# Attention with a top-32 mask and a gated expert layer: a different way to split double weights, and two weight pairs carried over from chunk to chunk

## Chip, cores and metric

One core of one Trainium2 chip. The metric is the device time of one execution in microseconds, the median of the runs.

## What is computed

```python
scores = scale * np.matmul(q, k.transpose(0, 1, 3, 2))        # 4 batches, 8 heads, 576 x 576, head size 64
kth = np.partition(scores, -32, axis=-1)[..., -32:-31]
scores = np.where(scores >= kth, scores, -1000000000.0)
attn = softmax(scores); x = attn @ v                          # 2304 tokens x 512
out = ((x @ w_a) * (x @ w_b)) @ w_out                         # 512 -> 1536 -> 512
```

The inputs q, k, v are float32; the three weight matrices are 64-bit doubles and reach the chip as such.

## The kernel before

**Matmuls.** A float32 product is made of fp32r products: each operand is split into a high part h (fp32r) and a low part l, and h·h + h·l + l·h are added in PSUM. Activations are split with a ScalarE copy (h) and a GpSimd subtraction (l).

**Attention.** The 2304 tokens are taken in 8 chunks (256 or 320 tokens of one batch), each chunk in 4 pairs of heads, each pair in 4 or 5 tiles of 128 query rows: 144 tiles. Per tile: TensorE makes the scores (L499, or L505 to L510), ScalarE copies half or all of them to SBUF (L526, L528), VectorE finds the 32 largest of each row with eight-at-a-time maxima (L535 to L545), ScalarE takes the exponential (L557, L570), the mask comes from VectorE (L559) or from a TensorE product (L568), the row is divided by its sum (p, L577 on GpSimd or L575 on ScalarE), TensorE transposes p (L601), ScalarE and GpSimd split it (L608 to L617), and TensorE multiplies by v (L647 to L662). From `SCALAR_SCALE` on, every even tile takes L575 in place of L577.

**Experts.** `up` makes, for a chunk, 24 products of x with a weight tile w (12 pairs of w_a and w_b; L697 to L699, 12 matmuls each); the pair is multiplied and split into gh and gl (L706 to L717). `down` makes 4 products with the 12 tiles of w_out, which stay in SBUF (L727 to L729, 36 matmuls each). A chunk's `up` and `down` are mixed with the attention of the chunk behind it; the last chunk's stand at the end.

**Conversion of the weights.** Each of the 36 weight tiles (128 x 512 doubles) goes once through `convert`: two loads of 512 KB, the raw words (L430, `raw`) and the same shifted by two bytes (L431, `alt`); two ScalarE Relu copies of the high words (L451, L452) that GpSimd adds (L453); VectorE shifts the bits in place and cuts them to h (L449), takes the next bits from `alt` (L449 again) and the exponent alone (L456); ScalarE writes h (L457) and turns the next bits into a float (L458); GpSimd multiplies it by the exponent's power of two, which is l (L459). The 24 tiles of w_a and w_b are then written to DRAM (`wd`, L461) and loaded again for every chunk (L693) through 4 buffers `w`. Of the first chunk, the tiles from `CONV_FIRST` on are used right where they were converted. Scratch of a conversion is three slots of the 12 that w_out's tiles take later (or slots of kx, qx, ptl, or a piece of gh or gl).

**Order.** No engine's order is written by hand. Each operation goes to a planner (`Plan`) with an engine, a cost in us and a key; the planner plays the program through with these costs and emits each engine's operations in the order in which they started there, the smallest key first among those ready. The keys of attention are the tile's number, of conversion `CONV_AT + CONV_STEP * k`, of experts late ones. All DMAs are issued in one queue on SP, in order. Where TensorE would stand still in the plan, the planner puts a filler matmul of 256 columns in (L288, `still`), up to a number of columns per stretch.

Line numbers here and in the profile are those of the kernel before.

Of the kernel before, what the change touches and what calls it, by code (L numbers as in the profile page):

```python
# [246 lines left out]
def attn_moe(ctx: ExitStack, tc, qT, kT, v, wa, wb, wo, out):  # L247
# [43 lines left out]
        return Buf(pool, shape, dtype, tag, bufs)  # L291

    def act(n, fn, r, w, ps=False, ptr=0, k=None):
        plan.op("ACT", n / 1200 + (0.065 if ps else 0.093) + 0.093 * ptr, key[0] if k is None else k, fn, r, w)

    def dve(n, fn, r, w, cost=None, k=None):
        plan.op("DVE", cost or (n + 66) / 960, key[0] if k is None else k, fn, r, w)

    def pool(n, fn, r, w, cost=None):
        plan.op("POOL", cost or 0.2 + n / 480, key[0], fn, r, w)  # L300

    def pe(cols, fn, r, w, rows=1.0, num=0, k=None):
        plan.op("PE", cols / 2353 + 0.009 * num, key[0] if k is None else k, fn, r, w, rows=rows)
# [104 lines left out]
    def convert(j, i):  # L408

        src = wo[j] if i == 2 else (wa, wb)[i][j].rearrange("p k e -> p (k e)")
        n = 2 * NJ + j if i == 2 else 2 * j + i
        if i == 2 and j in CONV_AWAY:
            raw, alt = buf([128, 1024], U4, "kx", 2), buf([128, 1024], U4, "ptl", 2)
            tmp, low = buf([128, 512], U4, "qx", 2), buf([128, 512], U4, "qx", 2)
            plan.enlist(raw, alt, tmp, low)
        elif n < CONV_FIRST and n % CONV_BIG == CONV_BIG - 1:
            big = buf([128, 3840], U4, ("gh", "gl")[n // CONV_BIG % 2], 1)  # L420
            raw, alt, tmp, low = [Part(big, *x) for x in ((0, 1024), (1024, 1024), (2048, 512), (2560, 512))]
        else:
            while i == 2 and len(listed) + 1 + 3 * sum(x not in CONV_AWAY for x in range(len(listed), j + 1)) > NJ:
                plan.enlist(fin[len(listed)])
                listed.append(fin[len(listed)])
            raw, alt, both = [buf([128, 1024], U4, "wo", NJ, const) for _ in range(3)]
            tmp, low = Part(both, 0, 512), Part(both, 512, 512)
            plan.enlist(raw, alt, both)
        first = [PR[0]["kr"], PR[0]["qr"]]
        dma(524e3, lambda: nc.sync.dma_start(raw[:, :], src.bitcast(U4)), [], [raw], after=first)  # L430
        dma(524e3, lambda: nc.sync.dma_start(alt[:, :].bitcast(U2)[:, 1:2048], src.bitcast(U2)[:, 0:2047]), [], [alt], after=first)  # L431
        if i == 2:
            w = fin[j]
            if j == NJ - 1:
                plan.enlist(*fin)
        else:
            w = buf([128, 2, 4, 128], FR, "w", 4)

        def odd(x):
            return x[:, :].rearrange("p (n t) -> p n t", t=2)[:, :, 1]  # L440

        def part(k):
# [5 lines left out]
        def bits(out, x, by, keep, how):  # L448
            return vec.tensor_scalar(out, x, by, keep, op0=how, op1=OP.bitwise_and)  # L449

        act(512, lambda: nc.scalar.activation(f(tmp), odd(raw).bitcast(FT), AF.Relu, scale=2.0 ** -116), [raw], [tmp])  # L451
        act(512, lambda: nc.scalar.activation(f(low), odd(raw).bitcast(FT), AF.Relu, scale=-2.0 ** -84), [raw], [low])  # L452
# [66 lines left out]
    def topk(i, s):  # L519

        alone = vector_mask(i)
        sb = buf([128, 2, HS], FT, "sb", 2)
        if alone:
            act(S, lambda: nc.scalar.activation(sb.ap, s[:, :, 0:HS], AF.Copy), [s], [sb], ps=True)  # L526
# [12 lines left out]

        def eight(r):  # L540
            return tb[:, g, 8 * r:8 * r + 8] if r else t8.ap
        for r in range(4):
            dve(HS + 8, lambda r=r: vec.max(eight(r), mx[:, g]), [(mx, g, 0), (mx, g, 1)], [tk[r]])  # L543
            if r < 3:
                dve(HS + 8, lambda r=r: vec.match_replace(mx[:, g], eight(r), mx[:, g], LOW), [tk[r]], [(mx, g, 0), (mx, g, 1)], 0.44)  # L545
            if r == 0:
                act(1, lambda: nc.scalar.activation(bias.ap, t8[:, 0:1], AF.Copy, scale=-0.125), [t8], [bias], k=URGENT)
        if g == GRP - 1:
            pool(g, lambda: nc.gpsimd.tensor_tensor(short[:, i - g:i + 1], tb[:, :, 31], mx[:, :, HS + 7], OP.subtract),
                 [(mx, x, y) for x in range(GRP) for y in (0, 1)] + [(tb, x, 3) for x in range(GRP)], [("short", i)])  # L550
        return bias, (tb, g, tk[3]), sb

    def softmax(i, s, found):
        bias, (tb, g, tok), sb = found
        pt, sm = buf([128, 2, HS], FT, "p", 2), buf([128, 2], FT, "sm", 3)
        if vector_mask(i):
            act(S, lambda: nc.scalar.activation(pt.ap, sb.ap, AF.Exp, bias=bias.ap, scale=0.125),  # L557
                [sb, bias], [pt], ptr=1)
            dve(S, lambda: vec.scalar_tensor_tensor(pt.ap, sb.ap, tb[:, g, 31:32], pt.ap, op0=OP.is_ge, op1=OP.mult,  # L559
                                                    accum_out=sm[:, 0:1]), [sb, tok], [pt, sm], 0.95)  # L560
# [120 lines left out]

    G, A, O = {}, {}, {}

    def up(c, j, which):
        n = chunks[c][2]
        xh, xl = X[c]
        if (c, j, which) in direct:
            w = direct.pop((c, j, which))
            wt = [(w, 0), (w, 1)]
        else:  # L690
            w = buf([128, 2, 4, 128], FR, "w", 4)
# [50 lines left out]
    for i, t in enumerate(tiles):  # L742
# [23 lines left out]
        if c == 0:  # L766
# [6 lines left out]
            for j in range(NJ):  # L773
                key[0] = ATTENTION + CONV_AT + 2 * NJ * CONV_STEP + CONV_LAST * j
                convert(j, 2)
                key[0] = EXPERTS
                while k < CONV_FIRST * (j + 1) / NJ:
                    up(c, k // 2, k % 2)
# [149 lines left out]
```

## Time and profile before

| | us |
|---|---|
| median of 3 runs | 931.04 (927.84 to 936.62) |
| the profiled execution, whole | 930.03 |
| its span, first to last instruction | 928.1 |
| TensorE busy in the span | 862.6 (of it fillers 66.7) |
| VectorE busy | 771.2 |
| ScalarE busy | 702.2 |
| GpSimd busy | 599.4 |

The span falls into four stretches. Up to about 25 us the first tiles start. From 25 to 250 us the weights are converted beside the attention of the first tiles. From 250 to 850 us attention and experts run mixed. Behind 850 us are left the `down` of the last but one chunk and the `up` and `down` of the last. The tables of stretches give, for each engine, busy microseconds and the number of instructions, then the clock that TensorE was granted as a share, the mean busy share of the 16 DMA engines and what they moved.

### The profile page before, as it was taken

How to read it: one execution, taken by the hardware profiler on the slowest of the kernel's cores; microseconds unless marked ns; L12 is line 12 of the kernel's file. 1: busy time of each engine (PE TensorE's matmuls, PEld its weight loads, DVE VectorE, ACT ScalarE, POOL GpSimd, SP SyncE). 2: the span in 40 equal slices, each digit the busy share in tenths (PEclk: the TensorE clock that was granted, in tenths of full speed). 3: DMA queues.
4: the chain of work that ended last, by engine and by line, in shares of the span. 5: the costliest groups of instructions: out<-in, count | busy, mean ns of one | idle time of the engine just before them, and what ended most of it. 6: DMA issues, size and time to landing. Idle time of an engine off the chain costs nothing.

```text
span 928.1 us, 18959 instructions
## 1 busy us (share of the span) xinstructions
PE 862.6 (93%) x5893; PEld 762.4 (82%) x5893; DVE 771.2 (83%) x2390; ACT 702.2 (76%) x1618; POOL 599.4 (65%) x706
## 2 busy tenths in 40 slices
PE   6887989999899899989998999988999999999998
PEld 3454557576789899988898999987999989999987
DVE  5889989989699899989998999989999989992010
ACT  4687878998877888878897888887888877772220
POOL 3365657877767777767777786777777786762120
PEclk8898989999999999999999999999999999999999
DMA  8698877987548884578548884689467774673580
GB/s 277 249 303 315 293 267 282 310 301 273 143 105 250 254 272 101 173 262 256 151 126 237 261 276 125 195 270 256 124 211 215 254 193 114 206 225 105 188 281 27
DMA packets 101581, 202.52 MB, mean 218 GB/s; under 512 B 17761, under 2 KB 55649, under 8 KB 101473
## 3 DMA queue, kind: packets, MB, share of 16 engines
q1 hardware_dynamic: 101472, 201.24, 68.8%
q8 instruction: 49, 0.80, 0.4%
q14 instruction: 60, 0.48, 0.2%
HBM read 157.93 MB, written 17.30 MB: 189 GB/s over the span
## 4 chain that ended last, share of the span: by engine, by line
PE 50%; DVE 14%; DMA 12%; ACT 10%; POOL 8%; issue 4%; SPq 2%; POOLq 0%; ACTq 0%; DVEq 0%
PE mm L697 6%; PE tp L601 6%; DMA w<-wd 5%; PE mm L699 5%; PE mm L698 5%; PE mm L727 4%; PE mm L729 4%; PE mm L728 4%; DVE mx L545 3%; DVE top L543 2%; POOL ptl L615 2%; PE mm L660 2%; DMA wo<-wa 2%; PE mm L288 2%; PE s L499 2%
## 5 line engine op out<-in xcount | busy, mean ns | idle before, releaser
L697 PE MATMUL mm<-xh,w 128*128 128x256 f32 (+1 forms) x768 | 240.3, 313 | 16.8 <-DMA w<-wd 9.4
L699 PE MATMUL mm<-xh,w 128*128 128x256 f32 (+1 forms) x768 | 228.1, 297 | 0.3 <-POOL w L459 0.3
L698 PE MATMUL mm<-xl,w 128*128 128x256 f32 (+1 forms) x768 | 228.1, 297 | 0.0
L615 POOL TENSOR_TENSOR ptl<-e,pth 128x512 fp32r<-128x512 f32 (+1 forms) x126 | 151.9, 1209 | 80.7 <-ACT e L613 65.7
L543 DVE MAX8 top<-mx 128x8 f32<-128x296 f32 x432 | 194.8, 457 | 2.0
L697 PEld LDWEIGHTS mm<-xh,w 128*128 128x128 f32 x768 | 146.1, 190 | 29.0 <-issue 8.9
L699 PEld LDWEIGHTS mm<-xh,w 128*128 128x128 f32 x768 | 146.1, 190 | 0.5 <-POOL w L459 0.5
L698 PEld LDWEIGHTS mm<-xl,w 128*128 128x128 f32 x768 | 146.4, 191 | 0.0
L545 DVE MATCH_REPLACE8 mx<-top,mx 128x296 f32<-128x296 f32 x288 | 129.5, 450 | 0.1
L608 ACT ACTIVATE pth<-tp 128x640 fp32r<-128x640 f32 (+3 forms) x160 | 102.5, 649 | 24.9 <-PE tp L601 23.1
L717 POOL TENSOR_TENSOR gl<-a,gh 128x256 fp32r<-128x256 f32 (+1 forms) x96 | 78.5, 819 | 62.4 <-ACT gh L716 59.3
L727 PE MATMUL mm<-gh,wo 128*128 128x256 f32 (+1 forms) x384 | 117.4, 306 | 0.5 <-ACT b L733 0.5
L601 PE MATMUL tp<-ident,p 128*128 128x128 f32 x720 | 107.0, 280 | 10.5 <-POOL p L577 4.3
L729 PE MATMUL mm<-gh,wo 128*128 128x256 f32 (+1 forms) x384 | 113.6, 296 | 0.0
L728 PE MATMUL mm<-gl,wo 128*128 128x256 f32 (+1 forms) x384 | 113.5, 296 | 0.0
L577 POOL TENSOR_SCALAR p<-p,sm 128x576 f32<-128x576 f32 x87 | 72.4, 832 | 54.5 <-DVE sm L573 46.4
L601 PEld LDWEIGHTS tp<-ident,p 128*128 128x128 f32 x720 | 83.4, 142 | 25.4 <-POOL p L577 12.3
L711 DVE TENSOR_TENSOR a<-mm,a 128x320 f32<-128x320 f32 (+1 forms) x84 | 38.4, 458 | 64.9 <-PE mm L699 63.5
L535 DVE TENSOR_TENSOR mn<-s,sb 128x288 f32<-128x288 f32 x144 | 64.2, 446 | 24.6 <-ACT sb L528 19.0
L613 ACT ACTIVATE e<-tp 128x640 f32<-128x640 f32 x113 | 79.6, 704 | 4.6 <-POOL pth L617 4.2
L727 PEld LDWEIGHTS mm<-gh,wo 128*128 128x128 f32 x384 | 72.7, 189 | 1.6 <-ACT b L733 0.7
L728 PEld LDWEIGHTS mm<-gl,wo 128*128 128x128 f32 x384 | 72.8, 190 | 0.0
(124 smaller groups left out, 2218.7 us busy)
## 6 DMA issues: line engine op xcount, KB each, us to landing
w<-wd SPq DMA_DIRECT2D x182, 512.0 KB, 4.7
wd<-w SPq DMA_DIRECT2D x24, 512.0 KB, 5.5
kr<-kT SPq DMA_DIRECT2D x24, 288.0 KB, 3.3
kx<-kh SPq DMA_DIRECT2D x48, 144.0 KB, 2.6
kx<-kr SPq DMA_DIRECT2D x48, 144.0 KB, 4.3
vr<-v SPq DMA_DIRECT2D x25, 256.0 KB, 4.0
wo<-wa SPq DMA_DIRECT2D x12, 512.0 KB, 7.4
wo<-wa SPq DMA_DIRECT2D x12, 511.8 KB, 8.0
```

The costliest lines, as they stand in the source:

```text
L543: dve(HS + 8, lambda r=r: vec.max(eight(r), mx[:, g]), [(mx, g, 0), (mx, g, 1)], [tk[r]])
L545: dve(HS + 8, lambda r=r: vec.match_replace(mx[:, g], eight(r), mx[:, g], LOW), [tk[r]], [(mx, g, 0), (mx, g, 1)], 0.44)
L601: nc.tensor.transpose(tp[:, kb, :], pf[:, k0:k0 + 128], ident)
L608: act(640 // len(dst), lambda bh=bh, to=to, fr=fr: nc.scalar.activation(bh[:, :, to], tp[:, :, fr], AF.Copy), [tp], [(bh, i)], ps=True)
L613: act(640, lambda: nc.scalar.activation(e.ap, tp.ap, AF.Copy), [tp], [e], ps=True)
L615: pool(512 // len(dst), lambda bh=bh, bl=bl, to=to, fr=fr: nc.gpsimd.tensor_tensor(bl[:, :, to], e[:, 0:4, fr], bh[:, 0:4, to].bitcast(FT) ...
L697: mm(ps[:, :n], w[:, 0, kb, :], xh[:, kb, :n], start=(kb == 0), stop=False)
L698: mm(ps[:, :n], w[:, 0, kb, :], xl[:, kb, :n], start=False, stop=False)
L699: mm(ps[:, :n], w[:, 1, kb, :], xh[:, kb, :n], start=False, stop=(kb == 3))
L727: mm(ps[:, :n], fin[j][:, 0, ms], gh[:, j, :n], start=(j == 0), stop=False)
L728: mm(ps[:, :n], fin[j][:, 0, ms], gl[:, j, :n], start=False, stop=False)
L729: mm(ps[:, :n], fin[j][:, 1, ms], gh[:, j, :n], start=False, stop=(j == NJ - 1))
```

## The change

Three things change, and with them the planner's numbers.

1. In `convert`, the shifted copy `alt` and its load are gone. VectorE only shifts (L454 of the changed kernel) and takes the exponent alone into `low` (L455); ScalarE writes h (L456); GpSimd subtracts h from the shifted value W (L457); VectorE multiplies the next 16 bits, read as 16-bit integers from the raw words, by 2^-36 and the exponent's power of two (L458); GpSimd adds both (L459). Scratch is two slots of 12 in place of three.
2. `up` keeps the w tiles of the last two pairs of a chunk (`KEEP`), and the next chunk begins with these pairs; the order of pairs turns around from chunk to chunk.
3. The division of even tiles goes to ScalarE from tile 80 on, before from tile 30 on. Sixteen tiles of the first chunk, before 14, are loaded again from DRAM.

```diff
-SCALAR_SCALE = 30
+SCALAR_SCALE = 80
-CONV_FIRST = 14
+CONV_FIRST = 16
-TURN, WEIGH, SPLIT = 1.5, 0, -2
-CONV_AT, CONV_STEP, CONV_LAST = -1, 1.4, 1
+TURN, WEIGH, SPLIT = 1.5, 1, -4
+CONV_AT, CONV_STEP, CONV_LAST = -1, 1.7, 0.5
...
-        plan.op("DVE", cost or (n + 66) / 960, key[0] if k is None else k, fn, r, w)
+        plan.op("DVE", cost or (n + 76) / 960, key[0] if k is None else k, fn, r, w)
-        plan.op("SP", nbytes / 345e3, key[0], fn, r, w, num=num, inner=inner, after=after)
+        plan.op("SP", nbytes / 310e3, key[0], fn, r, w, num=num, inner=inner, after=after)
...
-        dma(524e3, lambda: nc.sync.dma_start(alt[:, :].bitcast(U2)[:, 1:2048], src.bitcast(U2)[:, 0:2047]), [], [alt], after=first)
...
-        dve(0, lambda: bits(tmp[:, :], tmp[:, :], 3, 0xFFFFF000, OP.logical_shift_left), [], [tmp], 0.4)
-        dve(0, lambda: bits(low[:, :], odd(alt), 4, 0x1FFFFF, OP.logical_shift_right), [alt], [low], 0.4)
-        dve(0, lambda: vec.tensor_scalar(alt[:, 0:512], tmp[:, :], 0xFF800000, None, op0=OP.bitwise_and), [tmp], [alt], 0.4)
-        act(512, lambda: nc.scalar.activation(part(0), f(tmp), AF.Copy, scale=2.0 ** 32), [tmp], [(w, 0)])
-        act(512, lambda: nc.scalar.activation(f(low), low[:, :], AF.Copy), [], [low])
-        pool(512, lambda: nc.gpsimd.tensor_tensor(part(1), alt[:, 0:512].bitcast(FT), f(low), OP.mult), [alt, low], [(w, 1)])
+        dve(0, lambda: vec.tensor_scalar(tmp[:, :], tmp[:, :], 3, None, op0=OP.logical_shift_left), [], [tmp], 0.58)
+        dve(0, lambda: vec.tensor_scalar(low[:, :], tmp[:, :], 0xFF800000, None, op0=OP.bitwise_and), [tmp], [low], 0.54)
+        act(512, lambda: nc.scalar.activation(part(0), f(tmp), AF.Copy), [tmp], [(w, 0)])
+        pool(512, lambda: nc.gpsimd.tensor_tensor(f(tmp), f(tmp), part(0).bitcast(FT), OP.subtract), [(w, 0)], [tmp])
+        dve(0, lambda: vec.scalar_tensor_tensor(f(low), upper(raw), 2.0 ** -36, f(low), op0=OP.mult, op1=OP.mult), [raw], [low], 0.68)
+        pool(512, lambda: nc.gpsimd.tensor_tensor(part(1), f(tmp), f(low), OP.add), [tmp, low], [(w, 1)])
...
+        elif (j, which) in kept:
+            w = kept.pop((j, which))
+            wt = [w]
...
+        if last and c + 1 < len(chunks):
+            kept[j, which] = w
...
-            for j in range(NJ):
+            first = sorted({j for j, _ in kept}, reverse=c % 2 == 1)
+            rest = sorted(set(range(NJ)) - set(first), reverse=c % 2 == 1 and c > 1)
+            for n, j in enumerate(first + rest):
                 for which in range(2):
-                    up(c, j, which)
+                    up(c, j, which, n >= NJ - KEEP)
```

What this makes of the order is shown at three places. First VectorE, before, around the thirteenth tile: the three VectorE steps of one conversion (`wo_1241` is its scratch, `wo_1154` its shifted load) between the top-32 steps of a tile.

```order
L449 TENSOR_SCALAR wo_1241<-wo_1241 128x512
L543 MAX top_1202<-mx_1159 128x8
L449 TENSOR_SCALAR wo_1241<-wo_1154 128x512
L545 MATCH_REPLACE mx_1159<-top_1202,mx_1159 128x296
L456 TENSOR_SCALAR wo_1154<-wo_1241 128x512
```

The same in the changed kernel, near the same tile (`wo_1297` is the scratch, `wo_1228` the raw words).

```order
L454 TENSOR_SCALAR wo_1297<-wo_1297 128x512
L545 MATCH_REPLACE mx_1280<-t8_1399,mx_1280 128x296
L455 TENSOR_SCALAR wo_1297<-wo_1297 128x512
L543 MAX top_1343<-mx_1280 128x8
L573 RECIPROCAL sm_1412<-sm_1412 128x1
L458 SCALAR_TENSOR_TENSOR wo_1297<-wo_1228,wo_1297 128x512
```

Three VectorE steps stay three; the last of them now reads two SBUF tensors. Second GpSimd, before, around the fifteenth tile, where L577 is the division of p that a tile's transposes wait for, and L453 and L459 are conversion.

```order
L577 TENSOR_SCALAR p<-p,sm 128x576
L459 TENSOR_TENSOR w<-wo 128x512
L453 TENSOR_TENSOR wo<-wo 128x512
L577 TENSOR_SCALAR p<-p,sm 128x576
L459 TENSOR_TENSOR w<-wo 128x512
L549 TENSOR_TENSOR short<-top,mx 128x2
L453 TENSOR_TENSOR wo<-wo 128x512
L459 TENSOR_TENSOR w<-wo 128x512
L577 TENSOR_SCALAR p<-p,sm 128x576
```

And in the changed kernel, around the fourteenth tile, where L453, L457 and L459 are conversion.

```order
L577 TENSOR_SCALAR p<-p,sm 128x576
L457 TENSOR_TENSOR wo<-wo,w 128x512
L453 TENSOR_TENSOR wo<-wo 128x512
L459 TENSOR_TENSOR w<-wo 128x512
L549 TENSOR_TENSOR short<-top,mx 128x2
L457 TENSOR_TENSOR wo<-wo,w 128x512
L453 TENSOR_TENSOR wo<-wo 128x512
L577 TENSOR_SCALAR p<-p,sm 128x576
L459 TENSOR_TENSOR w<-wo 128x512
L457 TENSOR_TENSOR wo<-wo,w 128x512
L453 TENSOR_TENSOR wo<-wo 128x512
L459 TENSOR_TENSOR w<-wo 128x512
```

Between the two divisions shown there stand five steps of conversion; before two, then three. Third the DMA queue of SP, before, where the second chunk's `up` ends: the loads of w0 and w1 (`wd0_0` to `wd1_1`) for the third chunk stand between the loads of attention (kx, vr, kr).

```order
L309 DMA kx_4706<-kh_4696 64x576 x2
L309 DMA w_4716<-wd0_0_68 128x1024
L309 DMA kx_4706<-kr_4509 64x576 x2
L309 DMA w_4769<-wd0_1_69 128x1024
L324 DMA vr_4798<-v 128x4x128
L326 DMA vr_4798<-v 64x128 x2
L309 DMA w_4808<-wd1_0_70 128x1024
L309 DMA w_4836<-wd1_1_71 128x1024
L318 DMA kr_4857<-kT 128x576
```

In the changed kernel, at the same place, behind the second chunk's last two loads of w.

```order
L311 DMA w_4665<-wd11_0_90 128x1024
L311 DMA w_4726<-wd11_1_91 128x1024
L326 DMA vr_4756<-v 128x4x128
L328 DMA vr_4756<-v 64x128 x2
L320 DMA kr_4767<-kT 128x576
L311 DMA mid_96<-qh_4460 64x64 x4
L311 DMA mid_96<-qr_4344 64x64 x2
L322 DMA qr_4928<-qT 128x320
L326 DMA vr_5021<-v 128x4x128
L328 DMA vr_5021<-v 64x128 x2
```

No load of w stands there; the third chunk's first one comes 28 rows later, behind the four stores of the chunk's result.

## Rows read from the trace of the kernel before

**Rows 1.** Busy time of each engine, four stretches (start:end, length first)
```profile
core 0: us, PE busy (x) PEld busy (x) DVE busy (x) ACT busy (x) POOL busy (x), PEclk, DMA share, GB/s
25.00:250.00 225.00, 202.98 (x1125) 136.95 (x1122) 202.94 (x576) 190.25 (x444) 149.54 (x156) 0.96 0.79 276
250.00:850.00 600.00, 573.12 (x4181) 548.47 (x4182) 550.79 (x1763) 489.25 (x1123) 433.02 (x522) 0.99 0.68 202
850.00:865.00 15.00, 15.00 (x104) 15.00 (x104) 0.00 (x0) 0.88 (x2) 0.00 (x0) 1.00 0.09 34
865.00:905.00 40.00, 36.31 (x289) 34.89 (x288) 4.67 (x11) 9.63 (x24) 8.10 (x11) 1.00 0.79 267
```

**Rows 2.** The same stretches, the filler matmuls alone (PE, PEld)
```profile
25.00:250.00 225.00, 49.87 (x264) 24.62 (x261) 0.96 0.79 276
250.00:850.00 600.00, 9.60 (x52) 4.76 (x52) 0.99 0.68 202
```

**Rows 3.** Waits of TensorE, 250 to 928 us: total, times, longest
```profile
PE mm L697 <- DMA w<-wd: 9.2, 12, 1.6
PE tp L601 <- ACT e L613: 3.6, 3, 2.0
PE s L568 <- ACT r L563: 3.1, 3, 2.2
PE s L509 <- ACT p L570: 2.7, 2, 2.1
PE mm L697 <- ACT a L706: 2.2, 3, 1.2
PE tp L601 <- POOL p L577: 2.0, 5, 0.6
...
PEld tp L601 <- POOL p L577: 7.2, 19, 0.8
...
PEld mm L697 <- DMA w<-wd: 2.7, 2, 1.5
```

**Rows 4.** Waits of VectorE, 25 to 250 us
```profile
DVE mn L535 <- ACT sb L528: 9.3, 13, 2.0
DVE sm L573 <- ACT sm L572: 6.6, 7, 2.1
```

**Rows 5.** Groups on VectorE by shape (count, busy us, mean ns)
```profile
L559 DVE SCALAR_TENSOR_TENSOR p<-sb,top,p 128x576 f32<-128x576 f32 x63 | 62.8, 997 | 0.4 <-issue 0.3
L449 DVE TENSOR_SCALAR wo<-wo 128x512 uint32<-128x512 uint32 x52 | 32.4, 633 | 3.4 <-POOL wo L453 3.4
L456 DVE TENSOR_SCALAR wo<-wo 128x512 uint32<-128x512 uint32 x26 | 15.3, 587 | 0.0
```

**Rows 6.** Single lines on VectorE: shortest, median, longest ns
```profile
L559 DVE SCALAR_TENSOR_TENSOR p<-sb,top,p x63: 786/849/2225, 261.2 to 836.0; 128x576 f32<-128x576 f32 x63
L449 DVE TENSOR_SCALAR wo<-wo x52: 402/420/1536, 17.4 to 223.9; 128x512 uint32<-128x512 uint32 x52
L449 DVE TENSOR_SCALAR qx<-ptl x8: 408/752/1492, 36.3 to 244.9; 128x512 uint32<-128x512 uint32 x8
L535 DVE TENSOR_TENSOR mn<-s,sb x144: 427/447/459, 7.0 to 827.4; 128x288 f32<-128x288 f32 x144
```

**Rows 7.** Groups on GpSimd and ScalarE by shape
```profile
L577 POOL TENSOR_SCALAR p<-p,sm 128x576 f32<-128x576 f32 x87 | 72.4, 832 | 54.5 <-DVE sm L573 46.4 <-DMA wo<-wb 5.1 <-DMA kx<-kh 1.2
L459 POOL TENSOR_TENSOR w<-wo 128x512 fp32r<-128x512 f32 x22 | 28.1, 1277 | 19.1 <-ACT wo L458 7.0 <-DVE top L543 6.6 <-DVE sm L573 1.9
L575 ACT ACTIVATE p<-p,sm 128x576 f32<-128x576 f32 x57 | 44.2, 775 | 4.7 <-DVE sm L573 4.3
L458 ACT ACTIVATE wo<-wo 128x512 f32<-128x512 uint32 x26 | 16.2, 624 | 2.3 <-DVE wo L449 2.2
```

**Rows 8.** DMA issues: count, KB each, median us to landing
```profile
w<-wd SPq DMA_DIRECT2D x182, 512.0 KB, 4.7
...
wo<-wa SPq DMA_DIRECT2D x12, 512.0 KB, 7.4
wo<-wa SPq DMA_DIRECT2D x12, 511.8 KB, 8.0
```

More of the change, by code (lines that the diff above doesn't have):

```diff
@@ L21 @@
 LO, HI = 256, 320
+W_BUFS = 4
+KEEP = 2
 GRP = 2
@@ L293, in act @@
     def act(n, fn, r, w, ps=False, ptr=0, k=None):
-        plan.op("ACT", n / 1200 + (0.065 if ps else 0.093) + 0.093 * ptr, key[0] if k is None else k, fn, r, w)
+        plan.op("ACT", n / 1200 + (0.085 if ps else 0.11) + 0.075 * ptr + 0.035 * (n == 1), key[0] if k is None else k, fn, r, w)
     def dve(n, fn, r, w, cost=None, k=None):
-        plan.op("DVE", cost or (n + 66) / 960, key[0] if k is None else k, fn, r, w)
+        plan.op("DVE", cost or (n + 76) / 960, key[0] if k is None else k, fn, r, w)
     def pool(n, fn, r, w, cost=None):
@@ L302, in pe @@
     def pe(cols, fn, r, w, rows=1.0, num=0, k=None):
-        plan.op("PE", cols / 2353 + 0.009 * num, key[0] if k is None else k, fn, r, w, rows=rows)
+        plan.op("PE", cols / 2300 + 0.009 * num, key[0] if k is None else k, fn, r, w, rows=rows)
     def dma(nbytes, fn, r, w, num=1, inner=False, after=()):
-        plan.op("SP", nbytes / 345e3, key[0], fn, r, w, num=num, inner=inner, after=after)
+        plan.op("SP", nbytes / 310e3, key[0], fn, r, w, num=num, inner=inner, after=after)
     def move(dst, src):
@@ L415, in convert @@
         if i == 2 and j in CONV_AWAY:
-            raw, alt = buf([128, 1024], U4, "kx", 2), buf([128, 1024], U4, "ptl", 2)
-            tmp, low = buf([128, 512], U4, "qx", 2), buf([128, 512], U4, "qx", 2)
-            plan.enlist(raw, alt, tmp, low)
+            raw, tmp, low = buf([128, 1024], U4, "kx", 2), buf([128, 512], U4, "qx", 2), buf([128, 512], U4, "qx", 2)
+            plan.enlist(raw, tmp, low)
         elif n < CONV_FIRST and n % CONV_BIG == CONV_BIG - 1:
             big = buf([128, 3840], U4, ("gh", "gl")[n // CONV_BIG % 2], 1)
-            raw, alt, tmp, low = [Part(big, *x) for x in ((0, 1024), (1024, 1024), (2048, 512), (2560, 512))]
+            raw, tmp, low = [Part(big, *x) for x in ((0, 1024), (1024, 512), (1536, 512))]
         else:
-            while i == 2 and len(listed) + 1 + 3 * sum(x not in CONV_AWAY for x in range(len(listed), j + 1)) > NJ:
+            while i == 2 and len(listed) + 1 + 2 * sum(x not in CONV_AWAY for x in range(len(listed), j + 1)) > NJ:
                 plan.enlist(fin[len(listed)])
                 listed.append(fin[len(listed)])
-            raw, alt, both = [buf([128, 1024], U4, "wo", NJ, const) for _ in range(3)]
+            raw, both = [buf([128, 1024], U4, "wo", NJ, const) for _ in range(2)]
             tmp, low = Part(both, 0, 512), Part(both, 512, 512)
-            plan.enlist(raw, alt, both)
+            plan.enlist(raw, both)
         first = [PR[0]["kr"], PR[0]["qr"]]
         dma(524e3, lambda: nc.sync.dma_start(raw[:, :], src.bitcast(U4)), [], [raw], after=first)
-        dma(524e3, lambda: nc.sync.dma_start(alt[:, :].bitcast(U2)[:, 1:2048], src.bitcast(U2)[:, 0:2047]), [], [alt], after=first)
         if i == 2:
@@ L436, in convert, with upper @@
         else:
-            w = buf([128, 2, 4, 128], FR, "w", 4)
+            w = buf([128, 2, 4, 128], FR, "w", W_BUFS)
         def odd(x):
             return x[:, :].rearrange("p (n t) -> p n t", t=2)[:, :, 1]
+        def upper(x):
+            return x[:, :].bitcast(U2).rearrange("p (n t) -> p n t", t=4)[:, :, 1]
         def part(k):
@@ L446, in f @@
             return x[:, :].bitcast(FT)
[L448 to L452, printed above, removed]
+        act(512, lambda: nc.scalar.activation(f(tmp), odd(raw).bitcast(FT), AF.Relu, scale=2.0 ** -112), [raw], [tmp])
+        act(512, lambda: nc.scalar.activation(f(low), odd(raw).bitcast(FT), AF.Relu, scale=-2.0 ** -80), [raw], [low])
         pool(512, lambda: nc.gpsimd.tensor_tensor(f(tmp), f(tmp), f(low), OP.add), [low], [tmp])
-        dve(0, lambda: bits(tmp[:, :], tmp[:, :], 3, 0xFFFFF000, OP.logical_shift_left), [], [tmp], 0.4)
-        dve(0, lambda: bits(low[:, :], odd(alt), 4, 0x1FFFFF, OP.logical_shift_right), [alt], [low], 0.4)
-        dve(0, lambda: vec.tensor_scalar(alt[:, 0:512], tmp[:, :], 0xFF800000, None, op0=OP.bitwise_and), [tmp], [alt], 0.4)
-        act(512, lambda: nc.scalar.activation(part(0), f(tmp), AF.Copy, scale=2.0 ** 32), [tmp], [(w, 0)])
-        act(512, lambda: nc.scalar.activation(f(low), low[:, :], AF.Copy), [], [low])
-        pool(512, lambda: nc.gpsimd.tensor_tensor(part(1), alt[:, 0:512].bitcast(FT), f(low), OP.mult), [alt, low], [(w, 1)])
+        dve(0, lambda: vec.tensor_scalar(tmp[:, :], tmp[:, :], 3, None, op0=OP.logical_shift_left), [], [tmp], 0.58)
[4 more added lines that the diff above has]
+        pool(512, lambda: nc.gpsimd.tensor_tensor(part(1), f(tmp), f(low), OP.add), [tmp, low], [(w, 1)])
         if i < 2:
@@ L542, in topk @@
         for r in range(4):
-            dve(HS + 8, lambda r=r: vec.max(eight(r), mx[:, g]), [(mx, g, 0), (mx, g, 1)], [tk[r]])
+            dve(HS + 8, lambda r=r: vec.max(eight(r), mx[:, g]), [(mx, g, 0), (mx, g, 1)], [tk[r]], 0.393)
             if r < 3:
-                dve(HS + 8, lambda r=r: vec.match_replace(mx[:, g], eight(r), mx[:, g], LOW), [tk[r]], [(mx, g, 0), (mx, g, 1)], 0.44)
+                dve(HS + 8, lambda r=r: vec.match_replace(mx[:, g], eight(r), mx[:, g], LOW), [tk[r]], [(mx, g, 0), (mx, g, 1)], 0.453)
             if r == 0:
@@ L682, in attn_moe, with up @@
     G, A, O = {}, {}, {}
-    def up(c, j, which):
+    kept = {}
+    def up(c, j, which, last=False):
         n = chunks[c][2]
@@ L777, in attn_moe @@
                 while k < CONV_FIRST * (j + 1) / NJ:
-                    up(c, k // 2, k % 2)
+                    up(c, k // 2, k % 2, k >= CONV_FIRST - 2 * KEEP)
                     k += 1
```

6 lines of the change are left out of this document (3 added, 3 removed).

## The prediction

> **What bounds the kernel now.** I read the table of stretches first, then the waits of the engine that is busiest in each stretch, then the durations of what the change touches. In the table the reader is to see that no single engine is the bound. From 250 to 850 us TensorE works 573.1 of 600 us and VectorE 550.8 [rows 1]: both are nearly full, and what is left to win there is the 27 us in which TensorE stands still and the 9.6 us in which it multiplies fillers [rows 2]. From 25 to 250 us TensorE only looks full: 49.9 of its 203.0 us are fillers [rows 1, 2]. VectorE, with the same 202.9 of 225 us but no filler, sets the pace there, since each tile of attention and each conversion needs it; it stands still for 22 us, and 15.9 of them are two waits for ScalarE, for the scores' copy and for the sum [rows 4]. Behind 850 us VectorE has almost nothing left; TensorE finishes `down` and then the last chunk's 24 products of `up`, 36.3 of 40 us at a DMA share of 0.79 [rows 1].
>
> So the change has two prices to look at: what it costs VectorE before 250 us, and what it takes from TensorE's waits after it.
>
> **Conversion, 25 to 250 us.** 36 conversions. Removed per conversion: a load of 512 KB [rows 8], 18.9 MB in all; one ScalarE copy of 0.624 us [rows 7], 22.5 us in all; one VectorE shift. Added: one VectorE product of two SBUF tensors, one GpSimd operation.
>
> VectorE: the removed shift has a mean of 0.633 us, that of the exponent 0.587 [rows 5]; I take 0.61. The product isn't in the trace. The nearest row is L559, the same operation with two SBUF inputs over 576 elements, where the product has 512: its shortest is 0.786 and its mean 0.997 [rows 5, 6], times 512/576 that gives 0.70 and 0.89 us. It could be below 0.70 only if 16-bit input made it faster; the lowest I allow is the shift's own shortest, 0.40 [rows 6]. I take 0.85, near the mean, since GpSimd is busier here than beside L559. 36 x (0.85 - 0.61) = +8.6 us; bounds 36 x (0.40 - 0.61) = -8 and 36 x (0.89 - 0.61) = +10.
>
> GpSimd: 36 operations at 1.277 us [rows 7] are +46 us, so its share of the stretch goes from 149.5/225 = 0.66 to 195.5/225 = 0.87. That isn't a bound by itself, but the shifts show that they are held up while GpSimd works: the shortest is 0.402, the median 0.420, the longest 1.536 us [rows 6], and the mean 0.633 is 0.23 over the shortest. The operation that reads its scores from PSUM, L535, stays between 0.427 and 0.459 [rows 6]. If the excess grows with GpSimd's share, 0.23 becomes 0.30, for the 72 shifts and masks that remain +5 us. Bounds: 0 (another cause) and 72 x (0.752 - 0.61) = +10, if all ran like the median of the slower of the two forms in [rows 6].
>
> The Trainium skill, "GPSIMD Engine Reference", section "Key points", says that GpSimd shares its SBUF interfaces with VectorE and gets in the way of VectorE instructions that run in a two-port mode or read two SBUF tensors. By that rule the new product is a victim as well as the shifts, and the new subtraction a culprit. The trace agrees in that L449 and L559 spread and L535 doesn't [rows 6].
>
> ScalarE: 22.5 of its 190.3 us in this stretch go [rows 1, 7]. VectorE's waits for ScalarE are 15.9 us [rows 4]; I take 10 of them to be gone, bounds 0 and 16. What is late next is VectorE's own queue. The load that goes hides behind nothing that VectorE waits for: no DMA stands among its longest waits [rows 4], so I cost it at 0; what covers it is the distance between a load and its use, and if that cover were thin the loads, 7.4 and 8.0 us from issue to landing [rows 8], could give a microsecond or two.
>
> The order agrees with a slow start and a quick end: by the 18th tile the changed kernel has done 78 of the 108 VectorE steps of conversion, before 59, and TensorE 298 fillers, before 234; by the 36th tile both have done all 108, with 305 and 288 fillers. Sum of this stretch: +8.6 + 5 - 10 = +3.6 us; bounds -8 + 0 - 16 = -24 and +10 + 10 - 0 = +20.
>
> **Kept weights.** 28 loads at 7 borders of chunks go, and two more tiles of the first chunk are loaded again: 182 [rows 8] become 156. But the four kept tiles fill all four buffers, and four tiles is what the kernel before had loaded ahead in that place. While `down` runs, DMA has little to do: a share of 0.09 in the last one [rows 1]. So the load saved was hidden, and the fifth tile still waits for the first buffer. In the last `up` 20 tiles must come in either way, so I cost the 3.7 us in which TensorE stands still there [rows 1] at no gain. What goes is queue: before, the loads for the next chunk stand between attention's loads, now attention's stand first. TensorE's waits for w behind 250 us are 9.2 + 2.7 = 11.9 us [rows 3]; with 13 MB less and the loads planned at a slower rate I take two thirds to be gone, -8; bounds 0 and -12.
>
> **Division moved.** 25 divisions go from ScalarE, 0.775 us, to GpSimd, 0.832 us [rows 7], in tiles 30 to 80: -19 us there and +21 here. TensorE's waits for ScalarE (e, r, p, a) behind 250 us are 3.6 + 3.1 + 2.7 + 2.2 = 11.6 us; a third gone is -4, bounds 0 and -12. Its waits for p from GpSimd are 2.0 + 7.2 = 9.2 us over 24 times [rows 3]; as many more tiles as before lie there, of which I take less than half to wait as long: +4; bounds 0 and +9. Behind the waiting transpose, TensorE's own queue is held up: no later matmul passes.
>
> **Fillers behind the 36th tile.** 32 in place of 56. One costs 9.60/52 = 0.185 us [rows 2], so -4.4 us where the gap is really filled with work, 0 where it just stays empty.
>
> **Sum.** +3.6 - 8 - 4 + 4 - 4.4 = -8.8 us. On the profiled execution's 930.0 us that is 921; the median of the runs, 931.0, lies 1 us above, which I leave out. With the bounds: -24 - 12 - 12 - 4.4 = -52, and +20 + 9 = +29. A measurement of this kernel tells about 1% from no change.
>
> **Rivals.**
> *VectorE and GpSimd collide, slower.* The first stretch becomes GpSimd's: between two divisions stand up to seven of its conversion steps, 9 us at 1.277 [rows 7], and p waits behind them; VectorE's shifts run near 0.75 (median of the slower form, [rows 6]) and the product at 1.1. VectorE then pays 36 x (0.75 + 0.75 + 1.1) - 36 x 3 x 0.61 = +28 us, none of it covered, and of the later gains only half come: -6, with +4 for p. That is 930 + 28 - 6 + 4 = 956 at the worst; with half of the collision 942, which I take for its price. It decides from the point where a conversion's three VectorE steps take over 2.2 us together, against 1.83 now. For it: the longest shift of 1.5 us. Against it: the median of 0.420 [rows 6], so most shifts are not held up even at GpSimd's 0.66.
> By the Trainium skill's rule quoted above from "GPSIMD Engine Reference", section "Key points", this case is the one to expect.
> *The gains are hidden anyway, no change.* Kept tiles save loads that nobody waits for, and fillers vanish without work in their place; +3.6 stays, and the waits for w shrink by 4: 930. For it: VectorE at 550.8 of 600 us [rows 1] takes over as soon as TensorE waits less. Against it: the change gives the planner costs nearer to the trace (0.58 for the shift, where before it counted 0.4 and rows 5 have 0.633), and a plan that is nearer to the chip leaves shorter waits.
> *The waits go for good, much faster.* Every wait of TensorE for w and for ScalarE behind 250 us goes, 11.9 + 11.6 = 23.5 us, and VectorE's 15.9 us before it; with the product, the shifts and the fillers as in the sum that is 930 - 23.5 - 15.9 + 8.6 + 5 - 4.4 = 900. For it: both are waits that an earlier plan could have filled. Against it: VectorE has 49 us left between 250 and 850 [rows 1], and some of TensorE's waits for ScalarE are waits for VectorE's maxima one step on.
>
> **How the numbers follow.** The forecast with its neighbours (910 to 926): 0.45. No change (926 to 938): 0.27. Collision (over 938): 0.20. Much faster (under 910): 0.08. The bound of faster is 921.7: of the forecast's 0.45 about 0.35 lies under it, with 0.08 that is 0.43; the bound of slower, 940.3, leaves 0.19 to the collision; the rest, 0.38, is within 1%. The range for 8 in 10 is 906 to 944; the forecast's own is 910 to 926.
>
> **What would show it.** Right: the three VectorE groups of conversion near 0.65, 0.6 and 0.85 us; VectorE's waits for ScalarE before 250 us under 8 us; the first chunk's `down` no later than before; the waits for w behind 250 us under 5 us. Wrong: the product at over 1 us or the shifts at over 0.75; GpSimd's divisions among TensorE's longest waits; waits for w unchanged at 9 us; a first stretch longer by over 8 us.

## The result and the profile after

The changed kernel takes 939.0 us (934.6 to 942.5, 20 runs), the kernel before 934.5 in as many runs: a ratio of 1.0055, 95% interval 1.0035 to 1.0075. It is slower by half a per cent, where 1.1% faster was forecast. The profiled execution takes 937.6 us with a span of 935.8; the span before was 928.1, so the two traces lie 7.7 us apart where the medians lie 4.5 apart.

The table of stretches, changed kernel, columns as in [rows 1]:

```profile
25.00:250.00 225.00, 199.51 (x1055) 129.33 (x1054) 214.18 (x545) 160.31 (x379) 196.67 (x181) 0.92 0.58 190
250.00:850.00 600.00, 576.51 (x4221) 552.74 (x4222) 560.13 (x1795) 481.37 (x1122) 460.78 (x558) 1.00 0.64 183
850.00:865.00 15.00, 15.00 (x104) 15.00 (x103) 0.00 (x0) 1.32 (x3) 0.48 (x1) 1.00 0.07 23
865.00:905.00 40.00, 35.52 (x277) 34.18 (x276) 4.20 (x10) 8.04 (x20) 6.64 (x9) 1.00 0.76 252
```

Before 250 us VectorE is busy for 214.2 us where it was 202.9, and yet ends fewer instructions, 545 for 576. GpSimd works 196.7 us for 149.5, ScalarE 160.3 for 190.3, and DMA is at 0.58 for 0.79. From 250 to 850 us TensorE does more than before, 576.5 us for 573.1, and its fillers cost 5.9 us for 9.6.

How far attention is shows in the same stretches with VectorE's reciprocal alone, one per tile (changed kernel, L573: time, then the count of tiles):

```profile
0.00:135.00 135.00, 2.19 (x15) 0.87 0.67 224
135.00:250.00 115.00, 2.75 (x18) 0.96 0.49 156
```

and in the kernel before (L573):

```profile
0.00:135.00 135.00, 2.86 (x18) 0.89 0.81 285
135.00:250.00 115.00, 2.56 (x17) 1.00 0.78 267
```

33 tiles for 35. Read from the starts of this instruction, the 36th tile is reached at 267.5 us, before at 250.1; the 48th at 330.5 and 327.5; the last at 841.1 and 837.2. So 17.4 us are lost up to tile 36, where both kernels have all conversions behind them; 14.4 are made up by tile 48, of which 0.9 go again by the last tile; and 3.8 more are lost behind it, where the last `up` takes 42 us for 40. Part of what is made up is only work that lies elsewhere: between tiles 36 and 48 TensorE starts 243 matmuls of `up` and `down`, before 293, because 17 of `down` came earlier and 33 of `up` come later. At 573.1/4181 = 0.137 us per matmul [rows 1] that is an estimate of 7 of the 14 us.

VectorE's time up to tile 36 accounts for the whole loss: 245.1 us busy and 22.4 idle, before 215.3 and 34.8. The conversion's three steps are 97.8 of it, before 67.2; all its other work is the same, 147.3 and 148.1. From 25 to 135 us VectorE is busy for 109.8 of 110 us, before for 96.7.

Where the time went (changed kernel, the conversion's steps on VectorE by shape, as [rows 5], then single lines as [rows 6]):

```profile
L458 DVE SCALAR_TENSOR_TENSOR wo<-wo 128x512 f32<-128x512 uint16 x26 | 30.0, 1155 | 0.0
L454 DVE TENSOR_SCALAR wo<-wo 128x512 uint32<-128x512 uint32 x26 | 21.7, 834 | 2.5 <-POOL wo L453 2.5
L455 DVE TENSOR_SCALAR wo<-wo 128x512 uint32<-128x512 uint32 x26 | 18.4, 708 | 0.0
```
```profile
L454 DVE TENSOR_SCALAR wo<-wo x26: 407/861/1406, 16.9 to 209.9; 128x512 uint32<-128x512 uint32 x26
L458 DVE SCALAR_TENSOR_TENSOR wo<-wo x26: 665/1318/1718, 19.0 to 211.7; 128x512 f32<-128x512 uint16 x26
```

The shift's median has gone from 0.420 to 0.861 us; its shortest, 0.407, has hardly moved (0.402). The product costs 0.665 at its shortest and 1.318 at its median. Over all 36 conversions (the views count 26, those whose scratch is `wo`) the three steps take 97.9 us when their times are added, before 68.0.

The trace in order of time shows what lengthens them. VectorE around 105 us:

```profile
104.82 0.40 DVE L455 TENSOR_SCALAR wo<-wo 128x512 uint32<-128x512 uint32 x1
...
105.58 0.93 DVE L458 SCALAR_TENSOR_TENSOR wo<-wo 128x512 f32<-128x512 uint16 x1
106.44 0.46 DVE L543 MAX8 top<-mx 128x8 f32<-128x296 f32 x1
106.81 1.11 DVE L454 TENSOR_SCALAR wo<-wo 128x512 uint32<-128x512 uint32 x1
```

and GpSimd beside it:

```profile
104.87 0.41 POOL L549 TENSOR_TENSOR short<-top,mx 128x2 f32<-128x2 f32 x1
105.23 0.74 POOL L678 TENSOR_TENSOR xl<-xf,xh 128x256 fp32r<-128x256 f32 x1
105.92 1.72 POOL L457 TENSOR_TENSOR wo<-wo,w 128x512 f32<-128x512 f32 x1
```

The order of the starts decides. The mask starts at 104.82, before L549 on GpSimd does, and takes 0.40 us. The product starts while L678 runs; that ends at 105.97, and the product 0.54 us later, at 106.51. The shift starts while the new subtraction runs; that ends at 107.64, and the shift 0.28 us later, at 107.92. The maximum between them (one SBUF tensor in) takes its usual 0.46, and the subtraction, which started while the product ran, takes 1.72 where 1.27 is the rule.

All starts and ends of the changed kernel's trace say the same. No GpSimd operation runs at the start of 13 of the 72 shifts and masks and of 7 of the 36 products: these take 0.40 to 0.42 and 0.67 us, whatever GpSimd starts meanwhile. Of the 59 shifts and masks that start while one runs, 52 end 0.27 to 0.30 us after it; of the 29 such products, 27 end 0.53 to 0.56 us after it; all of the others but one met only its last 0.02 to 0.12 us. So a step of the conversion that starts while GpSimd works loses what is left of GpSimd's operation. 59 of 72 shifts and masks now start so, at 0.88 us on average, before 55 of 108 at 0.84. The price is mostly that more of them meet GpSimd.

VectorE's waits for ScalarE before 250 us (as [rows 4]) did shrink, from 15.9 to 7.7:

```profile
DVE mn L535 <- ACT sb L528: 5.3, 8, 1.4
DVE sm L573 <- ACT sm L572: 2.4, 5, 0.6
```

and TensorE's waits for w behind 250 us hardly, from 11.9 to 9.8 us (as [rows 3]):

```profile
PE mm L704 <- DMA w<-wd: 9.8, 11, 1.6
```

### The profile page after: what moved, and what is told of

Same layout as the page of the kernel before. It is cut to its first block, busy times and chain, and to the rows that moved or that the text cites. A ratio compares the mean times of both kernels' runs of the same rounds, so it can differ in the third digit from the quotient of the medians.

```text
span 935.8 us, 18869 instructions
## 1 busy us (share of the span) xinstructions
PE 865.9 (93%) x5886; PEld 762.5 (81%) x5886; DVE 794.6 (85%) x2390; ACT 666.6 (71%) x1557; POOL 676.3 (72%) x767
## 5 line engine op out<-in xcount | busy, mean ns | idle before, releaser
L704 PEld LDWEIGHTS mm<-xh,w 128*128 128x128 f32 x768 | 145.2, 189 | 31.9 <-issue 12.3
L724 POOL TENSOR_TENSOR gl<-a,gh 128x256 fp32r<-128x256 f32 (+1 forms) x96 | 82.3, 859 | 70.3 <-ACT gh L723 66.3
L577 POOL TENSOR_SCALAR p<-p,sm 128x576 f32<-128x576 f32 x112 | 93.9, 839 | 35.1 <-DVE sm L573 32.8
L601 PE MATMUL tp<-ident,p 128*128 128x128 f32 x720 | 107.7, 281 | 12.3 <-POOL p L577 10.0
L601 PEld LDWEIGHTS tp<-ident,p 128*128 128x128 f32 x720 | 84.6, 143 | 24.5 <-POOL p L577 17.4
L535 DVE TENSOR_TENSOR mn<-s,sb 128x288 f32<-128x288 f32 x144 | 64.0, 444 | 17.4 <-ACT sb L528 16.1
```

Source lines behind the costliest of these rows:

```text
L601: nc.tensor.transpose(tp[:, kb, :], pf[:, k0:k0 + 128], ident)
L704: mm(ps[:, :n], w[:, 0, kb, :], xh[:, kb, :n], start=(kb == 0), stop=False)
```

## The experiments

**Theory** (collision)**:** the conversion got dearer on VectorE because GpSimd's work lies beside it, and that reaches the end. **Rivals:** the early delay is swallowed and the new order costs behind 250 us; or one of the other parts (kept tiles, division, planner's numbers) costs. Ratios are to the kernel before, run beside each experiment, with 95% intervals; the changed kernel has 1.0055. Tile 36 and the like are read from the starts of VectorE's reciprocal.

### One step of the conversion cut short, order unchanged

sub_short, on GpSimd:

```diff
-nc.gpsimd.tensor_tensor(f(tmp), f(tmp), part(0).bitcast(FT), OP.subtract)
+nc.gpsimd.tensor_tensor(f(tmp)[:, 0:8], f(tmp)[:, 0:8], part(0)[:, 0:8].bitcast(FT) if i == 2 else w[:, 0, 0, 0:8].bitcast(FT), OP.subtract)
```

> The changed kernel with the added GpSimd subtraction cut to 8 of 512 columns, same order on every engine (the low part of the weights then lacks W - h outside these columns). Collision theory (GpSimd's added work holds up VectorE's conversion steps, and the delay reaches the end): VectorE's three conversion groups fall from 97.9 us to 65 to 80, tile 36 is done by 250 to 258 us instead of 268, and the whole takes 929 to 934. Order theory (the early delay is swallowed, the end is set by the new order behind 250 us): tile 36 may come earlier, the whole stays at 937 to 941.

Measured: 927.0 us, 0.9937 (0.9904 to 0.9970). VectorE's three steps take 84.9 us, over the 65 to 80 expected; tile 36 is reached at 255 us. This run and the next leave out part of the weights' low part.

prod_short, on VectorE:

```diff
-vec.scalar_tensor_tensor(f(low), upper(raw), 2.0 ** -36, f(low), op0=OP.mult, op1=OP.mult)
+vec.scalar_tensor_tensor(f(low)[:, 0:8], upper(raw)[:, 0:8], 2.0 ** -36, f(low)[:, 0:8], op0=OP.mult, op1=OP.mult)
```

> The changed kernel with the VectorE product cut to 8 of 512 columns, same order on every engine (the low part of the weights then lacks most of its next bits). Collision theory: about 36 us of VectorE's 97.9 go, tile 36 is done by 248 to 256 us, the whole takes 928 to 934, since what VectorE loses before 250 us reaches the end in part. Order theory: tile 36 earlier, the whole within 2 us of the changed kernel (937 to 941).

Measured: 927.9 us, 0.9951 (0.9921 to 0.9981). The three steps take 77.5 us, tile 36 is at 258. Only 20 us go where 36 were expected, since a product of 8 columns, 0.14 to 0.17 us when GpSimd is idle at its start (10 of 36), still waits out GpSimd's operation otherwise and ends 0.02 us behind it. Its mean is 0.51 us (prod_short, by shape):

```profile
L458 DVE SCALAR_TENSOR_TENSOR wo<-wo 128x8 f32<-128x8 uint16 x26 | 13.3, 513 | 0.0
L454 DVE TENSOR_SCALAR wo<-wo 128x512 uint32<-128x512 uint32 x26 | 22.1, 849 | 2.9 <-POOL wo L453 2.9
```

In both, the order of every engine is that of the changed kernel, and the shortened step takes 1.0 to 1.2% off the whole. VectorE's time up to tile 36, in us:

| | three steps | its other work | idle | tile 36 at | span |
|---|---|---|---|---|---|
| before | 67.2 | 148.1 | 34.8 | 250.1 | 928.1 |
| changed | 97.8 | 147.3 | 22.4 | 267.5 | 935.8 |
| sub_short | 84.8 | 147.7 | 22.3 | 254.8 | 921.5 |
| prod_short | 77.4 | 148.3 | 32.1 | 257.8 | 927.0 |

In sub_short all that VectorE saves comes off tile 36 (13 of 13 us); in prod_short half of it does (10 of 20), and the other half becomes idle time, as VectorE now waits for ScalarE (23.7 us up to tile 36 for the copy and the sum, 14.4 in the changed kernel). In both, what comes off tile 36 comes off the end: 13 and 10 us there, 14 and 9 in the span, 11 and 10 by the ratios. The order rival, by which an early delay is swallowed, falls. And GpSimd's step costs as much as VectorE's own. In sub_short VectorE's shift got shorter, though nothing about it was changed (by shape):

```profile
L458 DVE SCALAR_TENSOR_TENSOR wo<-wo 128x512 f32<-128x512 uint16 x26 | 23.5, 904 | 0.0
L454 DVE TENSOR_SCALAR wo<-wo 128x512 uint32<-128x512 uint32 x26 | 18.1, 696 | 2.6 <-POOL wo L453 2.6
```

### The conversion and the rest of the change, one without the other

old_conv puts `convert` as it was before (shifted copy, three scratch slots, steps at planner costs of 0.58, 0.58, 0.54) into the changed kernel; new_conv puts the new `convert` into the kernel before.

```diff
-        raw, both = [buf([128, 1024], U4, "wo", NJ, const) for _ in range(2)]
+        raw, alt, both = [buf([128, 1024], U4, "wo", NJ, const) for _ in range(3)]
...
+        dma(524e3, lambda: nc.sync.dma_start(alt[:, :].bitcast(U2)[:, 1:2048], src.bitcast(U2)[:, 0:2047]), [], [alt], after=first)
```

> The changed kernel with the conversion of before (shifted copy, three VectorE shifts and masks, two GpSimd steps), with the new planner numbers, kept pairs and moved divisions. Collision theory: VectorE's conversion groups near 68 us, tile 36 by 245 to 255 us, whole 926 to 934, not slower than before. Order theory: whole 937 to 942, as the changed kernel, since the order is what costs.

> The kernel before with the new conversion alone (old planner numbers for the rest, no kept pairs, divisions on ScalarE from tile 30). Collision theory: VectorE's conversion groups 90 to 100 us, tile 36 by 262 to 272 us, whole 936 to 944. Order theory: whole 929 to 935, as before.

| | rest as before | rest as changed |
|---|---|---|
| conversion as before | 1 | 0.9949 (0.9911 to 0.9988), 927.3 us |
| conversion as changed | 1.0281 (1.0238 to 1.0324), 960.7 us | 1.0055 (1.0035 to 1.0075), 939.0 us |

The new conversion costs 1.1% with the rest as changed and 2.8% with the rest as before. The rest gains 0.5% with the old conversion and 2.2% with the new. The planner orders each of the four anew, so these differences hold the price of another order too. new_conv is slower than either theory had it; VectorE's steps take 99.5 us there, as expected, and tile 36 comes at 271, but another 10 us are lost behind the last tile, and its span ends 30 us after that of before. There its last `up` begins before the `down` ahead of it and takes 61 us for 40; no_keep, old_conv_no_keep, divide_30, old_costs, old_keys, divide_early_act and both_mends have the same order at the end. old_conv is faster than both kernels: it reaches 35 tiles by 250 us (its reciprocal is L575),

```profile
0.00:135.00 135.00, 2.86 (x18) 0.99 0.84 293
135.00:250.00 115.00, 2.65 (x17) 1.00 0.71 244
```

with the DMA load of the shifted copy back at shares of 0.84 and 0.71. So the copy that went had cost nothing that these runs show.

### The other parts, one taken back at a time

Each is the changed kernel with one line or one set of numbers of before.

```diff
-KEEP = 2
+KEEP = 0
```

> The changed kernel without kept weight tiles: every chunk loads its 24 tiles, 182 loads in place of 156 to 158; else as changed. Theory of hidden loads (the four tiles were loaded ahead while the DMA queue had nothing to do): within 0.4% of the changed kernel, 935 to 942 us, TensorE's waits for w near 10 us as with kept tiles. Rival (kept tiles spare waits and pay back part of the early loss): 941 to 948, waits for w over 14 us.

Measured: 940.9 us, 1.0101 (1.0063 to 1.0138). That is 0.5% over the changed kernel, give or take 0.4; TensorE's waits for w are 12.2 us, for 9.8 with kept tiles. A small loss, at the edge of what these runs can tell, and the other order at the end can be part of it.

The same edit on old_conv instead of the changed kernel:

> The conversion of before in the changed kernel, without kept tiles. Theory of hidden loads: within 0.4% of the same with kept tiles (927.3), 924 to 931 us. Rival (kept tiles are what beats the kernel before): 931 to 936.

Measured: 936.9 us, 1.0047 (1.0017 to 1.0077), so with the old conversion the kept tiles are worth 1%, against the theory of hidden loads. Its order is planned anew, and at tile 144 it stands at 835 us in its profile, old_conv at 834; the last `up` takes 61 us for 40, since it begins before the `down` ahead of it. How much of the 1% is spared loading and how much another order isn't settled.

```diff
-SCALAR_SCALE = 80
+SCALAR_SCALE = 30
```

> The changed kernel with even tiles' division on ScalarE from tile 30 on, as before. If GpSimd's extra divisions cost what it hides elsewhere: 934 to 941 us, no change over 0.4%. If moving them to GpSimd is what pays back between tiles 36 and 48: the stretch from tile 36 to 48, 62 us in the changed kernel, goes back towards the 78 us of before, whole 943 to 952. If it costs: 928 to 934.

Measured: 940.5 us, 1.0082 (1.0050 to 1.0114). Tiles 36 to 48 take 69 us, 6 more than in the changed kernel, but the whole shows no difference that these runs tell.

```diff
-        plan.op("DVE", cost or (n + 76) / 960, key[0] if k is None else k, fn, r, w)
+        plan.op("DVE", cost or (n + 66) / 960, key[0] if k is None else k, fn, r, w)
...
-TURN, WEIGH, SPLIT = 1.5, 1, -4
+TURN, WEIGH, SPLIT = 1.5, 0, -2
```

The first stands for all of the planner's costs (old_costs), the second, with CONV_STEP 1.4 and CONV_LAST 1, for its keys (old_keys).

> The changed kernel with the planner's costs of before (shift and mask 0.4, maxima, PSUM and DMA figures); conversion, kept tiles and keys as changed. If the planner's costs are what pays back between tiles 36 and 48: tile 36 stays near 268 us, tiles 36 to 48 take 70 to 80 us in place of 62, whole 946 to 958, towards the 960.7 of the new conversion in the old order. If not: 935 to 943.

> The changed kernel with the keys of before (WEIGH 0, SPLIT -2, CONV_STEP 1.4, CONV_LAST 1); costs as changed. If the earlier split and load of the next pair (SPLIT -4) is what pays back between tiles 36 and 48: whole 945 to 956, with waits of ScalarE for qr back at 4 to 5 us between 250 and 340. If not: 935 to 943.

Measured: old_costs 996.6 us, 1.0693 (1.0656 to 1.0731); old_keys 951.0 us, 1.0193 (1.0151 to 1.0235). With the costs of before the plan loses 6.3% on the changed kernel, more than expected and not where expected: tiles 36 to 48 take 59 us, no more than in the changed kernel. Tile 36 comes 12 us later, at 279.5, and 34 us more are left behind the last tile (129 for 95), since TensorE works 550.7 us of the 600 between 250 and 850 for 576.5:

```profile
250.00:850.00 600.00, 550.69 (x3968) 517.10 (x3967) 555.59 (x1774) 475.39 (x1109) 446.04 (x544) 0.99 0.60 171
```

old_keys lies in the range that its expectation had for the earlier split, but not for that reason: tiles 36 to 48 take 63 us, as in the changed kernel. Against that kernel it is 5 us late at tile 36 and 10 at tile 144.

### Attempts to mend it

true_conv_costs gives the planner costs near what the three steps take in the trace (0.77, 0.66 and 1.04 us; their means, 0.853, 0.740 and 1.127, are 0.08 or 0.09 longer, about what one VectorE operation overlaps the next in the lines around 105 us); divide_early_act moves 36 divisions off GpSimd while it converts; both_mends does both.

```diff
-        dve(0, lambda: vec.scalar_tensor_tensor(f(low), upper(raw), 2.0 ** -36, f(low), op0=OP.mult, op1=OP.mult), [raw], [low], 0.68)
+        dve(0, lambda: vec.scalar_tensor_tensor(f(low), upper(raw), 2.0 ** -36, f(low), op0=OP.mult, op1=OP.mult), [raw], [low], 1.04)
...
-        if i >= SCALAR_SCALE and i % 2 == 0:
+        if i < 36 or i >= SCALAR_SCALE and i % 2 == 0:
```

> The changed kernel with the planner's costs of the three VectorE conversion steps set to what its own trace shows (0.77, 0.66, 1.04 in place of 0.58, 0.54, 0.68). VectorE's work stays the same. If part of the loss is that the order was made for shorter steps: 929 to 935 us, tile 36 earlier than 268. If only the work counts: 936 to 942, VectorE's conversion groups still 95 to 100 us.

> The changed kernel with the divisions of tiles 0 to 35 on ScalarE instead of GpSimd: 36 operations of 0.84 us leave GpSimd while the weights are converted. Collision theory (what counts is how long GpSimd works beside VectorE's two-port steps): VectorE's conversion groups fall from 97.9 to 85 to 92 us, tile 36 by 258 to 264, whole 928 to 935. Rival (only the two-input GpSimd operations of the conversion collide, the division has one tensor input): groups stay at 95 to 100 us, whole 935 to 942.

> Early divisions on ScalarE and the true costs of the conversion steps together. If both mends work and add up: 924 to 932 us, level with the conversion of before in the new order (927.3). If neither does: 936 to 942.

Measured: true_conv_costs 954.2 us, 1.0237 (1.0201 to 1.0274); divide_early_act 945.4, 1.0155 (1.0113 to 1.0198); both_mends 952.2, 1.0201 (1.0168 to 1.0234). None mends, all are slower than the changed kernel, and why a plan with truer costs is worse stays open. divide_early_act says something about the collision all the same: GpSimd's busy time before 250 us falls from 196.7 to 165.5 us, yet the three steps take 101.9 us. GpSimd's total doesn't decide, then, but what it is at when a step starts: fewer shifts and masks start while it works, 50 for 59, yet those take 0.94 us for 0.88, and 30 products 1.40 for 1.24.

### One input in place of two, order unchanged

```diff
-nc.gpsimd.tensor_tensor(f(tmp), f(tmp), part(0).bitcast(FT), OP.subtract)
+nc.gpsimd.tensor_scalar(f(tmp), part(0).bitcast(FT), 0.0, 1.0, op0=OP.mult, op1=OP.mult)
```

> The changed kernel with the added GpSimd subtraction replaced by a GpSimd multiplication of one tensor by constants over the same 512 columns, same order on every engine (W - h is then left out of the low part). By the division's row it takes 0.65 to 0.75 us in place of 1.27, so GpSimd loses 20 us of 46. Two-input theory (only GpSimd operations with two tensor inputs collide with VectorE's shifts, masks and product): VectorE's conversion groups fall from 97.9 to 82 to 88 us, as with the subtraction cut to 8 columns (84.9), tile 36 by 253 to 260 us, whole 925 to 931. Busy theory (any GpSimd work collides, by its length): groups at 89 to 94 us, tile 36 by 260 to 264, whole 930 to 936.

Measured: 931.2 us, 0.9983 (0.9953 to 1.0014); the three steps take 89.7 us, tile 36 is at 261. The step itself takes 0.617 us at its median:

```profile
L457 POOL TENSOR_SCALAR wo<-w x22: 607/617/1059, 20.9 to 158.0; 128x512 f32<-128x512 f32 x22
```

That lies in the bands of the busy theory, between cutting the step and leaving it. So one input isn't harmless: of the products with this step alone beside them, eight, half take 0.67 to 0.68 us and half 0.96 to 1.02. The starts tell them apart. The four long ones start 0.13 to 0.20 us after the step and end 0.54 us after its end; of the short ones three start before it, and one 0.13 us before its end. Beside a division alone, five products take 0.67 to 0.69, and all five start before the division, by 0.18 to 0.19 us; where a division runs at the product's start (two cases) the product ends 0.54 us after it as well. With two inputs (changed kernel, the subtraction alone beside them) three of seven take 1.66 and more, and they start 0.15 us after it. So neither the inputs nor the kind of GpSimd's step decides in these runs, but which of the two starts first and how long GpSimd's has still to run: 0.62 us in all with one input, 1.27 with two.

## Why the prediction was wrong

*The bound.* Right: VectorE sets the pace before 250 us, and a delay at tile 36 arrives at the end, as sub_short and prod_short show. TensorE's fillers don't cover it. Close behind VectorE stands its wait for ScalarE: in prod_short that takes back half of what VectorE is spared.

*The conversion on VectorE.* This step failed. "I take 0.85" for the product, and "+5 us" for the shifts and masks, made +13.6; measured are 1.127 on average over 36, which is 36 x (1.127 - 0.641) = +17.5, and 36 x (0.853 + 0.740 - 0.641 - 0.609) = +12.3: +29.9 us. GpSimd's share came out as worked out, 196.7/225 = 0.87. What was wrong was to let the excess over the shortest grow with GpSimd's share, from 0.23 to 0.30 us: it went to 0.39, because the shifts and masks that start while GpSimd works went from 55 in 108 to 59 in 72, and each of them pays 0.48 us over the shortest, before 0.44. For the product, 29 of 36 start so, at 1.24 us. The 0.85 came from L559, which runs where GpSimd is less busy. The rival named for this, collision, had the price of the steps right (+28 us; 2.6 us per conversion, measured 2.72) and its place; it was given 0.20. That its 942 lies near the 939.0 is in part luck: it counts half of that price and no cover, where VectorE paid all of it and 12.4 us less of idle time covered part.

The Trainium skill's rule in "GPSIMD Engine Reference", section "Key points", that GpSimd contends with VectorE instructions in a two-port mode or with two SBUF inputs, had named the victims. The trace agrees: shifts (0.407 to 1.406 us) and product (0.665 to 1.718) stretch, the maxima (0.44 to 0.47) don't.

*The cover.* Right in size: 8.2 of 15.9 us of waits for ScalarE went, 10 were taken. The load that went was worth nothing, as priced: old_conv has it and is faster than both kernels. With +29.9 in place of +13.6 the prediction's own sum for the first stretch is +29.9 - 10 = +20; the trace has +17.4, made of +29.8 busy and -12.4 idle on VectorE.

*Kept tiles.* "Two thirds gone, -8" was too much: -2.1 us in the waits. As the working had said just before, the loads were mostly hidden. In the whole the kept tiles are worth 0.5% with the new conversion, give or take 0.4, and 1% with the old one, the other order included.

*Division.* Nothing that divide_30 can tell, as summed (-4 + 4), but not by these terms: behind 250 us TensorE's waits for p fell, from 9.2 to 4.6 us, where +4 was taken. They rose in the place that the sum left out, before 250 us, from 7.4 to 22.7 us, as the collision rival had said (p waits behind the conversion's steps on GpSimd). 17.2 of the 22.7 lie before 135 us, where VectorE has no time to spare anyway (109.8 of 110 us from 25 on); whether the rest sets the pace between 135 and 250 us, where VectorE stands still for 10.6 us, no run separates.

*Fillers.* -3.7 us, -4.4 forecast.

*What the sum lacked.* The planner's numbers stood in it only as a reason against a rival. They are the largest lever of all: with the new conversion the costs alone are worth 6%, and the new conversion without any of the rest is 2.8% slower. So the result's nearness to no change is made of two larger effects against each other. Which part of the order wins its share back isn't shown: no run puts it between tiles 36 and 48, where it seemed to lie.

## What to carry to other kernels

A step moved to GpSimd because GpSimd has time isn't free where VectorE is the bound: look in the trace for VectorE operations whose shortest and longest lie far apart, count how many start while GpSimd works now and how many would, and price those at what is left of GpSimd's operation then, beside their own time. Where a planner orders the work, a comparison of two versions of a step holds only with the order kept: shrink the step and keep its planned cost, as sub_short does. And taking away a transfer whose landing nobody waits for is no gain, however large it is.

## What the runs showed that was not expected

One GpSimd operation per conversion cost 1.2% of the whole (1.0055 against 0.9937 in sub_short), largely by making VectorE slower at its own work: 13 us of VectorE's conversion went with it. VectorE's step waits out the GpSimd operation that runs when it starts, and goes through untouched where it starts first. It works both ways: the subtraction takes 1.39 us on average, where the conversion's GpSimd steps took 1.28 to 1.30 before.

```profile
L457 POOL TENSOR_TENSOR wo<-wo,w 128x512 f32<-128x512 f32 x22 | 30.5, 1389 | 1.9 <-DVE wo L455 1.8
```

The order alone moved the time by up to 6% at the same work (old_costs against the changed kernel), and truer costs for three steps made it 1.8% worse.

The fastest version found that leaves nothing out is old_conv, the old conversion with the rest of the change: 0.9949 of the kernel before (0.9911 to 0.9988).
